# One routing group of eight units at the head of a fused attention and expert kernel

## The chip, the cores and the metric

The kernel runs on one core of a Trainium2 chip. The core has TensorE (PE, with its weight loads PEld), VectorE (DVE), ScalarE (ACT), GpSimd (POOL) and SyncE (SP); each takes its instructions in the order in which they are written, and waits for the others by semaphores. SP and POOL also issue DMAs. The metric is the device time of one execution, in microseconds (us).

## The reference

An attention with exponential gates over 4 x 8 sequences of 768 steps gives 3072 rows of 320; these go through a mixture of eight experts, two for each row.

```python
def _attn_ref(q, k, v, i_gate, f_gate, o_gate):
    ...
    for t in range(S):
        m_new = np.maximum(f_gate[:, :, t] + m, i_gate[:, :, t])
        f_stab = np.exp(f_gate[:, :, t] + m - m_new)
        i_stab = np.exp(i_gate[:, :, t] - m_new)
        ...
        y[:, :, t] = o * h_tilde / denom

def _moe_ref(x, w_gate, w_noise, noise, w1, w2):
    logits = x @ w_gate
    noise_scale = np.log1p(np.exp(x @ w_noise))
    noisy_logits = logits + noise_scale * noise
    top2 = np.argpartition(-noisy_logits, 2, axis=1)[:, :2]
    top2_l = np.take_along_axis(noisy_logits, top2, axis=1)
    top2_l = top2_l - top2_l.max(-1, keepdims=True)
    top2_w = np.exp(top2_l)
    top2_w /= top2_w.sum(-1, keepdims=True) + 1e-09
    ...
            h = np.maximum(x[mask] @ w1[e], 0.0)
            out[mask] += top2_w[mask, k, None] * (h @ w2[e])
```

## The kernel before

**Attention.** The steps are cut into chunks of 64 and the batch into two pairs, which makes 24 units of 128 rows. A loop with one iteration for each unit `i` (0 to 21; 22 and 23 are written out behind it) issues the work of several units at once: `k_part(i + 1)` (`kd`, L367), `c_part(i)` (the state, `st` L387, copied by L390), `o_part(i)` (L396), `e_part(i + 2)` (the gates' exponentials, `e` L336 and `w` L339), `f_part(i)` (`dn` L401 and L403, `tm` L407, then `xr` on GpSimd, L408), `p_part(i + 1)` (`p`, L373, or L377 where a sequence starts), `s_part(i + 2)` (L359), and for the unit before, the transposes L419, their copy L423 and the logits L439. `XR` rows are written to DRAM by `keep_rows`. In the same loop the first expert's weights come in: at the ends of iterations 11, 13, 17, 19, 20 and 21 ScalarE rounds a piece (`w1h`) and GpSimd subtracts it (`w1l`, L147).

**Routing.** `g_part(g)` is a generator that routes a group of units (four before). It starts when the group's last unit has its logits. Its steps: softplus of the noise (L542; three activations that `act` issues, L719; L551 to L561), noisy logits (L564), MAX8 for each unit (L569), the search of its indices for each unit (L572), one-hots (L579), counts (`m` L585, L588 or L590; `base` by a scan, L593), weights (L602, L604), and then, when TensorE has added the counts (`want`, `r_part`, L448 to L450), the rank of every row in its expert's list (L614, L630), split into a column `ai`, `ah` and a place `bi` (L634 to L642), and two tables of one-hot factors, `OA` (L649, L652) and `OB` (L655). A burst of eight matmuls (`b_part`, L459) multiplies these and adds them to the table `TBL` that says which rows an expert takes. `done` counts the units that are in it.

**What sets the order.** `fill` issues steps of the waiting generators, four times in an iteration: a little after `kd`, after each of the `dn` steps, and at the end up to a share of 1.6 for an iteration (a step counts as 0.19, MAX8 0.1, a search 0.15, the products 0.3, 0.3 and 0.6). `lag` says how many units later a burst or a count may be issued. When 12 units are in the table, `decode` (L473 to L490) makes row numbers of the first expert's first 384 places and `gather` (L803, GpSimd) fetches these rows in two iterations, two tiles and one. When 20 and 24 are in it, the same is done for the other places.

**Expert 0.** Behind the loop `mm1(0, 0, f)` runs for eight `f` (L1031), with routing in between by `advance`, and then three passes of 24 matmuls each into `sums` (L1154), eight for each of three tiles; `low_w2` (L1128) makes the low half of its second weights beside them. In the third pass the gathered tiles 3 and 4 are transposed (L833) for `mm1(0, 1, f)`. The other seven experts follow.

Of the kernel before, what the change touches and what calls it, by code (L numbers as in the profile page):

```python
# [10 lines left out]
HF = mybir.dt.float16  # L11
# [3 lines left out]
OP = mybir.AluOpType  # L15
# [3 lines left out]
NE, F, DM = 8, 1024, 320  # L19
# [8 lines left out]
TC = BLK // 128  # L28
# [5 lines left out]
FIT = 2048  # L34
FF = 1024
NM = 768
GROUPS = tuple((u, 4) for u in range(0, 24, 4))
GOF = {u: g for g, (u0, n) in enumerate(GROUPS) for u in range(u0, u0 + n)}
NB = 4

EF, LONG = 2, 3
NR = NE - EF
# [25 lines left out]
def build(ctx, tc, qk, vk, og, fi, noise, wgn, w1, w2, cst, ce, out):  # L68
    nc = tc.nc
    V, A, P, T, SP = nc.vector, nc.scalar, nc.gpsimd, nc.tensor, nc.sync  # L70
# [14 lines left out]
    spot = keep.tile([128, 128, 2], HF, name="spot")  # L85
    cols = keep.tile([128, NE * TC, 2], HF, name="cols")
    sgn = keep.tile([128, 2 * NU], HF, name="sgn")
# [422 lines left out]
    def lc_part(i, t, w):  # L510
        u = i - 2
        if 0 <= u < NU:
            g = GOF[u]
            c = u - GROUPS[g][0]
            if c == 0:
                LG[g] = rt.tile([128, NB, 16], F32, name="lg")
            A.activation(LG[g][:, c, :], t[:, LGC:LGC + 16], AF.Copy)
# [6 lines left out]
    anew = {}  # L524
    for nb in sorted({n for _, n in GROUPS}):
        anew[nb] = rt.tile([128, NE, nb + 1], BF, name=f"anew_{nb}", bufs=1)
        P.memset(anew[nb], 1.0)
        P.memset(anew[nb][:, :, 0], 0.0)
    bursts, done, acts, lag = [], [0], [], [1, 1]
    OBT = [rt.tile([128, 4, 128, 2], HF, name=f"ob{i}", bufs=1) for i in range(2)]  # L530
    OAT = [rt.tile([128, 4, NE * TC, 2], HF, name=f"oa{i}", bufs=1) for i in range(2)]

    def g_part(g):

        u0, nb = GROUPS[g]
        lg = LG[g][:, 0:nb]
        f = lambda a: a.rearrange("p u e -> p (u e)")
        fe = lambda a: a.rearrange("p e u -> p (e u)")
        sm = lambda name, shape, dt=F32: rt.tile(shape, dt, name=f"{name}_{nb}", bufs=1)
# [93 lines left out]
        ai = sm("ai", [128, 2 * nb], I32)  # L633
        V.tensor_scalar(ai, f(r), 7, None, op0=OP.arith_shift_right)  # L634
        yield
        n = 2 * nb
        assert n == 8
        bi = sm("bi", [128, n], HF)
        V.scalar_tensor_tensor(bi, ai, -128.0, f(r), op0=OP.mult, op1=OP.add)
        yield  # L640
        ah = sm("ah", [128, n], HF)
        V.tensor_copy(ah, ai)  # L642
        while done[0] < u0 - 4:
            yield "wait"
        OB, OA = OBT[g % 2], OAT[g % 2]
        C = NE * TC
        yield "long"
        two = lambda a, c: a.rearrange("p (a b) -> p a b", b=2)[:, :, None, :].to_broadcast([128, 4, c, 2])
        V.tensor_tensor(OA, cols[:, None].to_broadcast([128, 4, C, 2]), two(ah, C), op=OP.is_equal)  # L649
        yield 0.3  # L650
        yield "long"
        V.tensor_mul(OA, OA, two(sgn[:, 2 * u0:2 * u0 + n], C))  # L652
        yield 0.3
        yield "long"
        V.tensor_tensor(OB, spot[:, None].to_broadcast([128, 4, 128, 2]), two(bi, 128), op=OP.is_equal)  # L655
        yield 0.6
        bursts.append(([OB[:, j // 2, :, j % 2] for j in range(n)], [OA[:, j // 2, :, j % 2] for j in range(n)], unit[0] + lag[1]))
        if u0 + nb == NU:
            V.tensor_add(rk[:, 0:1], rk[:, 0:1], bump[0])
            yield  # L660
# [37 lines left out]
    spent, long = [0.0], set()  # L698
# [48 lines left out]
    def route(i):  # L747
        if 2 <= i <= NU + 1 and sum(GROUPS[GOF[i - 2]]) == i - 1:
            routing.append(g_part(GOF[i - 2]))
# [91 lines left out]
    unit = [0]  # L841
# [3 lines left out]
    while i < NU - LEAD:  # L845
# [33 lines left out]
        if i in (6, 7):  # L879
            n = slice(64 * (i - 6), 64 * (i - 6) + 64)  # L880
# [52 lines left out]
    u = NU - 2  # L933
# [19 lines left out]
    u = NU - 1  # L953
# [197 lines left out]
    for k, (l, r) in enumerate(((HH, W2H), (HLO, W2H), (HH, W2L))):  # L1151
        for n in range(24):
            t, j = divmod(n, 8)
# [261 lines left out]
```

## Time and profile before

| | |
|---|---|
| three executions | 512.7, 514.81, 516.75 us, median 514.81 |
| span of the profiled execution | 512.4 us (its own time outside the span is not recorded) |
| busy TensorE, VectorE, ScalarE, GpSimd | 97%, 65%, 48%, 45% of the span |
| granted TensorE clock | 0.986 |

The span runs from the first instruction to the last. Times in the rows are counted from its start. A busy share is an average over two stages: the attention loop takes the first 127 us, the experts the rest.

### The profile page before, as it was taken

How to read it: one execution, taken by the hardware profiler on the slowest of the kernel's cores; microseconds unless marked ns; L12 is line 12 of the kernel's file. 1: busy time of each engine (PE TensorE's matmuls, PEld its weight loads, DVE VectorE, ACT ScalarE, POOL GpSimd, SP SyncE). 2: the span in 40 equal slices, each digit the busy share in tenths (PEclk: the TensorE clock that was granted, in tenths of full speed). 3: DMA queues.
4: the chain of work that ended last, by engine and by line, in shares of the span. 5: the costliest groups of instructions: out<-in, count | busy, mean ns of one | idle time of the engine just before them, and what ended most of it. 6: DMA issues, size and time to landing. Idle time of an engine off the chain costs nothing.

```text
span 512.4 us, 13150 instructions
## 1 busy us (share of the span) xinstructions
PE 497.5 (97%) x5043; PEld 472.3 (92%) x5043; DVE 331.3 (65%) x935; ACT 245.7 (48%) x584; POOL 231.1 (45%) x303
## 2 busy tenths in 40 slices
PE   8899999998999999999999999999999999999995
PEld 4698888887999988999999999999999999999994
DVE  8868889889787586754853675375448347555410
ACT  7768888898623355423531543154235315514300
POOL 9736666265113876156135605531561354151033
PEclk9969999999999999999999999999999999999998
DMA  6888787877767465296159417723941682372033
GB/s 168 237 224 259 211 245 207 228 209 230 260 217 234 108 98 180 46 242 157 30 100 271 104 28 195 171 79 68 278 90 39 162 203 80 65 169 26 2 36 45
DMA packets 51493, 76.89 MB, mean 150 GB/s; under 512 B 10825, under 2 KB 41808, under 8 KB 51392
## 3 DMA queue, kind: packets, MB, share of 16 engines
q1 hardware_dynamic: 38576, 50.16, 33.7%
q0 software_dynamic: 12848, 25.82, 24.0%
q8 instruction: 42, 0.69, 0.6%
q14 instruction: 27, 0.22, 0.1%
HBM read 52.10 MB, written 17.32 MB: 135 GB/s over the span
## 4 chain that ended last, share of the span: by engine, by line
PE 83%; DVE 8%; DMA 4%; ACT 2%; issue 1%; POOL 1%; SPq 1%; POOLq 0%; DVEq 0%
PE s L1031 25%; PE e L1031 12%; PE o L1066 5%; PE o L1065 5%; PE o L1064 5%; PE st L1066 5%; PE st L1065 5%; PE st L1064 5%; PE o L396 3%; DVE p L373 2%; PE e L336 2%; PE s L359 1%; PE s L1154 1%; PE xt L439 1%; PE st L387 1%; DVE kd L367 1%
## 5 line engine op out<-in xcount | busy, mean ns | idle before, releaser
L1087 POOL DMA_INDIRECT y_out<-y,tok x53 | 87.2, 1646 | 178.6 <-DVE y L1077 177.5
L1044 ACT ACTIVATE hx<-s 128x384 fp32r<-128x384 f32 (+5 forms) x91 | 43.5, 478 | 72.7 <-PE s L1031 67.9
L1031 PE MATMUL s<-xh,w1h 128*128 128x384 f32 (+6 forms) x273 | 76.0, 336 | 0.0
L803 POOL DMA_INDIRECT xg<-rows,tok x53 | 56.3, 1062 | 35.7 <-issue 13.7
L1047 DVE SCALAR_TENSOR_TENSOR hx<-s,hx 128x384 fp32r<-128x384 f32 (+3 forms) x91 | 48.1, 528 | 34.2 <-ACT hx L1044 34.0
L1031 PE MATMUL s<-xh,w1l 128*128 128x384 f32 (+6 forms) x273 | 61.9, 334 | 0.0
L1066 PE MATMUL o<-w2h,hx 128*128 128x320 f32 x184 | 56.9, 309 | 0.0
L1064 PE MATMUL o<-w2h,hx 128*128 128x320 f32 x184 | 56.8, 309 | 0.0
L1065 PE MATMUL o<-w2l,hx 128*128 128x320 f32 x184 | 56.8, 309 | 0.0
L1066 PE MATMUL st<-w2h,hx 128*128 128x320 f32 x176 | 54.4, 309 | 0.0
L1064 PE MATMUL st<-w2h,hx 128*128 128x320 f32 x176 | 54.4, 309 | 0.0
L1065 PE MATMUL st<-w2l,hx 128*128 128x320 f32 x176 | 54.3, 309 | 0.0
L1031 PEld LDWEIGHTS s<-xh,w1h 128*128 128x128 f32 x273 | 48.8, 188 | 1.3 <-ACT xh L835 0.3
L1031 PEld LDWEIGHTS s<-xh,w1l 128*128 128x128 f32 x273 | 47.8, 188 | 1.1 <-DVE xh L837 0.2
L1031 PE MATMUL s<-xl,w1h 128*128 128x384 f32 (+6 forms) x182 | 46.0, 334 | 0.0
L1044 ACT ACTIVATE hx<-e 128x384 fp32r<-128x384 f32 (+5 forms) x45 | 21.7, 482 | 48.9 <-PE e L1031 36.2
L1077 DVE TENSOR_SCALAR y<-o,gw 128x320 f32<-128x320 f32 x23 | 12.7, 550 | 45.8 <-PE o L1066 45.8
L1077 DVE TENSOR_SCALAR y<-st,gw 128x320 f32<-128x320 f32 x22 | 12.1, 551 | 43.3 <-PE st L1066 43.3
L1031 PE MATMUL e<-xh,w1h 128*128 128x384 f32 (+6 forms) x135 | 38.4, 338 | 0.0
L408 POOL TENSOR_TENSOR xr<-tm,vk 128x320 f32<-128x320 f32 x24 | 20.9, 871 | 35.3 <-ACT w L339 10.4
L345 ACT ACTIVATE vk<-vk 128x320 f32<-128x320 f32 x72 | 33.8, 471 | 2.8 <-DMA vk<-og_in 1.9
L1064 PEld LDWEIGHTS o<-w2h,hx 128*128 128x128 f32 x184 | 34.5, 188 | 0.0
(247 smaller groups left out, 1242.1 us busy)
## 6 DMA issues: line engine op xcount, KB each, us to landing
raw<-w_in SPq DMA_DIRECT2D x6, 1280.0 KB, 6.9
qk<-qk_in SPq DMA_DIRECT2D x24, 256.0 KB, 3.9
raw<-w_in SPq DMA_DIRECT2D x6, 1024.0 KB
y_out<-zrow SPq DMA_DIRECT2D x15, 320.0 KB, 4.2
raw<-w_in SPq DMA_DIRECT2D x17, 256.0 KB, 7.7
vk<-vk_in POOLq DMA_DIRECT2D x24, 162.0 KB, 3.9
vk<-vk_in SPq DMA_DIRECT2D x24, 162.0 KB, 4.0
vk<-og_in SPq DMA_DIRECT2D x24, 160.0 KB, 3.6
```

The source lines that it names most:

```text
L345: A.activation(g, g, (AF.Exp, AF.Ln, AF.Exp)[p], bias=float(p == 1), scale=(-1.0, 1.0, -1.0)[p])
L396: T.matmul(OQ[u][half[p], h, :], PP[u][n, p, h, :], VK[u % 4][p][n, h * 41:h * 41 + 41], start=True, stop=True)
L408: P.tensor_mul(XR[u], tm.rearrange("p h d -> p (h d)"), SG[u % 4])
L803: P.indirect_dma_start(out=XG[0:rows_of(e, t), t], out_offset=None, in_=XD[0:n], in_offset=bass.IndirectOffsetOnAxis(ap=token(e, t), axis= ...
L1031: T.matmul(ps[:, 0:n], l, r, start=i == 0, stop=i == len(ops) - 1)
L1044: A.activation(hi, x, AF.Relu)
L1047: V.scalar_tensor_tensor(lo, top[0], 0.0, top[1].bitcast(F32), op0=OP.max, op1=OP.subtract)
L1064: T.matmul(ps, HH[:, j, c], W2H[:, j], start=j == 0, stop=False)
L1065: T.matmul(ps, HH[:, j, c], W2L[:, j], start=False, stop=False)
L1066: T.matmul(ps, HLO[:, j, c], W2H[:, j], start=False, stop=j == 7)
L1077: V.tensor_scalar(y[0:n], ps[0:n], GW[e][0:n, t:t + 1], None, op0=OP.mult)
L1087: st = P.indirect_dma_start(out=out, out_offset=bass.IndirectOffsetOnAxis(ap=token(e, t), axis=0), in_=y[0:n], in_offset=None, compute_op= ...
```

## The change

The first eight units become one group. Its steps are issued once, on tiles twice as wide; MAX8 and the search stay one for each unit. The tables `OA` and `OB` are still made for four units at a time, so the group makes two pairs and two bursts, and the second half waits until its buffer is free. Groups after the first are as before. The tile of logits (`lg`) is eight units wide for all groups.

```diff
-GROUPS = tuple((u, 4) for u in range(0, 24, 4))
+GROUPS = ((0, 8), (8, 4), (12, 4), (16, 4), (20, 4))
 GOF = {u: g for g, (u0, n) in enumerate(GROUPS) for u in range(u0, u0 + n)}
-NB = 4
+NB = 8
...
-        while done[0] < u0 - 4:
-            yield "wait"
-        OB, OA = OBT[g % 2], OAT[g % 2]
...
+        C, n = NE * TC, 8
         two = lambda a, c: a.rearrange("p (a b) -> p a b", b=2)[:, :, None, :].to_broadcast([128, 4, c, 2])
...
+        for uh in range(u0, u0 + nb, 4):
+            while done[0] < uh - 4:
+                yield "wait"
+            OB, OA = OBT[uh // 4 % 2], OAT[uh // 4 % 2]
+            own_ = slice(2 * (uh - u0), 2 * (uh - u0) + n)
+            yield "long"
+            V.tensor_tensor(OA, cols[:, None].to_broadcast([128, 4, C, 2]), two(ah[:, own_], C), op=OP.is_equal)
+            yield 0.3
+            yield "long"
+            V.tensor_mul(OA, OA, two(sgn[:, 2 * uh:2 * uh + n], C))
+            yield 0.3
+            yield "long"
+            V.tensor_tensor(OB, spot[:, None].to_broadcast([128, 4, 128, 2]), two(bi[:, own_], 128), op=OP.is_equal)
+            yield 0.6
+            bursts.append(([OB[:, j // 2, :, j % 2] for j in range(n)], [OA[:, j // 2, :, j % 2] for j in range(n)], unit[0] + lag[1]))
```

VectorE, iteration 13, from `tm` of unit 13 on; before:

```order
L407 SCALAR_TENSOR_TENSOR tm<-dn,o 128x320
L373 TENSOR_TENSOR p<-s,w 128x1024
L655 TENSOR_TENSOR ob_217<-spot,bi_1641 128x1024
L542 SCALAR_TENSOR_TENSOR na_1741<-lg 128x32
L367 TENSOR_TENSOR kd<-vk_114,w 128x640
L401 RECIPROCAL dn<-o 128x8
L551 SCALAR_TENSOR_TENSOR co_1806<-t_4_1744,ue_1743 128x32
L403 SCALAR_TENSOR_TENSOR dn<-dn 128x8
```

and in the changed kernel:

```order
L407 SCALAR_TENSOR_TENSOR tm<-dn,o 128x320
L373 TENSOR_TENSOR p<-s,w 128x1024
L614 TENSOR_TENSOR oh_1479<-oh_1479,rk_1531 128x128
L630 TENSOR_REDUCE rank<-oh_1479 128x16
L634 TENSOR_SCALAR ai_1674<-rank 128x16
L637 SCALAR_TENSOR_TENSOR bi_1676<-ai_1674,rank 128x16
L640 CAST ah_1678<-ai_1674 128x16
L649 TENSOR_TENSOR oa_221<-cols,ah_1678 128x448
L652 TENSOR_TENSOR oa_221<-oa_221,sgn 128x448
L655 TENSOR_TENSOR ob_219<-spot,bi_1676 128x1024
L367 TENSOR_TENSOR kd<-vk_114,w 128x640
L542 SCALAR_TENSOR_TENSOR na_1696<-lg 128x32
```

The rank and the first half of the tables of the wide group stand there now, and the next group's first step stands behind `kd`.

TensorE, the passes into `sums` behind the attention; `ob` are the burst's factors of units 16 to 19. Before:

```order
L1154 MATMUL s_3008<-w2h,hx 128x320 x8
L1154 MATMUL s_3009<-w2h,hx 128x320 x8
L1154 MATMUL e<-w2h,hx 128x320 x8
L1154 MATMUL s_3008<-w2h,hx 128x320 x4
L459 LDWEIGHTS ob_216
L459 MATMUL o<-oa_218,ob_216 128x56
```

and in the changed kernel:

```order
L1154 MATMUL s_2962<-w2h,hx 128x320 x8
L1154 MATMUL s_2963<-w2h,hx 128x320 x8
L1154 MATMUL e<-w2h,hx 128x320 x8
L1154 MATMUL s_2962<-w2h,hx 128x320 x8
L1154 MATMUL s_2963<-w2h,hx 128x320 x8
L1154 MATMUL e<-w2h,hx 128x320 x2
L459 LDWEIGHTS ob_219
L459 MATMUL o<-oa_221,ob_219 128x56
```

The burst stood behind 4 matmuls of the second pass; now it stands behind 18.

VectorE at the same place, from that burst's `ob` to the decode. Before:

```order
L655 TENSOR_TENSOR ob_216<-spot,bi_3000 128x1024
L561 TENSOR_TENSOR ln_2934<-ln_2934,nzt 128x32
L564 TENSOR_TENSOR nl_3033<-ln_2934,lg 128x32
L569 MAX mx_3035<-nl_3033 128x8 x4
L466 TENSOR_TENSOR tbl<-tbl,o 128x56
```

and in the changed kernel:

```order
L655 TENSOR_TENSOR ob_219<-spot,bi_2956 128x1024
L561 TENSOR_TENSOR ln_2904<-ln_2904,nzt 128x32
L564 TENSOR_TENSOR nl_2991<-ln_2904,lg 128x32
L1128 TENSOR_TENSOR w2l<-raw_122,w2h 128x320 x3
L569 MAX mx_3012<-nl_2991 128x8 x3
L1128 TENSOR_TENSOR w2l<-raw_122,w2h 128x320
L466 TENSOR_TENSOR tbl<-tbl,o 128x56
```

Four subtractions for `w2l` stand ahead of the addition to the table now.

## Rows read from the trace of the kernel before

**Rows 1.** The page, the chain of work that ended last, by engine.

```profile
PE 83%; DVE 8%; DMA 4%; ACT 2%; issue 1%; POOL 1%; SPq 1%; POOLq 0%; DVEq 0%
```

**Rows 2.** Stretches: start:end, length, busy time of each engine (instructions), clock, DMA.

```profile
43.74:49.74 6.00, 5.93 (x126) 5.06 (x124) 4.27 (x12) 5.42 (x18) 3.83 (x7) 1.00 0.86 237
49.74:72.84 23.10, 22.23 (x531) 20.07 (x530) 19.55 (x74) 18.90 (x52) 16.03 (x32) 1.00 0.84 231
72.84:83.24 10.40, 9.73 (x233) 8.52 (x235) 9.88 (x31) 8.35 (x22) 6.86 (x12) 1.00 0.78 217
83.24:88.00 4.76, 4.53 (x119) 4.20 (x119) 4.53 (x9) 4.44 (x13) 2.71 (x3) 1.00 0.71 219
88.00:111.54 23.54, 23.14 (x573) 20.73 (x575) 20.48 (x81) 20.14 (x55) 9.91 (x15) 1.00 0.79 207
111.54:117.47 5.93, 5.09 (x122) 4.43 (x126) 5.83 (x18) 4.54 (x12) 5.30 (x6) 1.00 0.94 292
117.47:126.87 9.40, 8.31 (x217) 7.37 (x210) 8.99 (x20) 8.83 (x22) 5.38 (x6) 1.00 0.68 196
126.87:155.87 29.00, 29.00 (x234) 27.77 (x232) 22.18 (x106) 14.53 (x43) 6.49 (x10) 1.00 0.69 224
```

**Rows 3.** Chain of waits: start, time on the chain, what; two neighbouring `o` bursts.

```profile
38.09 0.93 PE o L396 x32
...
42.49 0.93 PE o L396 x32
```

**Rows 4.** VectorE's groups, 39.34 to 126.87: busy us, mean ns, idle before.

```profile
L373 DVE TENSOR_TENSOR p<-s,w 128x1024 f32<-128x1024 f32 x18 | 21.9, 1216 | 0.0
L367 DVE TENSOR_TENSOR kd<-vk,w 128x640 f32<-128x640 f32 x16 | 12.9, 809 | 0.0
L407 DVE SCALAR_TENSOR_TENSOR tm<-dn,o 128x320 f32<-128x320 f32 x18 | 8.5, 473 | 1.0
...
L655 DVE TENSOR_TENSOR ob<-spot,bi 128x1024 f16<-128x1024 f16 x4 | 2.7, 682 | 0.0
...
L649 DVE TENSOR_TENSOR oa<-cols,ah 128x448 f16<-128x448 f16 x4 | 1.6, 392 | 0.1
...
L553 DVE RECIPROCAL na<-t 128x32 f32<-128x32 f32 x4 | 1.4, 345 | 0.0
...
L579 DVE TENSOR_TENSOR oh<-cs,mi 128x64 f32<-128x64 f32 x4 | 0.9, 221 | 0.0
...
L551 DVE SCALAR_TENSOR_TENSOR co<-t,ue 128x32 f32<-128x32 f32 x4 | 0.8, 192 | 4.2 <-ACT t L719 4.1
L557 DVE TENSOR_TENSOR ln<-ln,co 128x32 f32<-128x32 f32 x4 | 0.8, 192 | 0.4
```

**Rows 5.** VectorE's timeline: start, duration, instruction; two of the four long ones.

```profile
75.52 1.28 DVE L585 TENSOR_TENSOR m<-oh 128x32 bf16<-128x32 f32 x1
...
113.44 2.25 DVE L575 TENSOR_TENSOR d<-mx 128x4 f32<-128x4 f32 x1
```

**Rows 6.** GpSimd's timeline, three of the six subtractions; idle before in brackets.

```profile
75.41 1.28 POOL L147 TENSOR_TENSOR w1l<-raw,w1h 128x512 fp32r<-128x512 f32 x1 [0.81 <-ACT w1h L144]
...
85.50 1.36 POOL L147 TENSOR_TENSOR w1l<-raw,w1h 128x512 fp32r<-128x512 f32 x1 [0.49 <-ACT w1h L144]
...
104.51 1.56 POOL L147 TENSOR_TENSOR w1l<-raw,w1h 128x512 fp32r<-128x512 f32 x1 [1.14 <-ACT w1h L144]
```

**Rows 7.** TensorE's timeline in the passes into `sums`.

```profile
148.12 0.39 PE L459 MATMUL o<-oa,ob 128*128 128x56 f16 x8
148.34 2.01 PE L1154 MATMUL s<-w2h,hx 128*128 128x320 f32 x12
...
153.56 0.49 PE L833 MATMUL s<-cs,xg 128*128 128x128 f32 x3
```

**Rows 8.** GpSimd's timeline: the first gather for tiles 3 and 4.

```profile
150.00 1.03 POOL L803 DMA_INDIRECT xg<-rows,tok  x1 [10.12 <-DVE km L490]
```

**Rows 9.** DMA issues, 149.5 to 153: kind, count, median us from issue to landing.

```profile
xg<-rows,tok POOLq DMA_INDIRECT x2, 3.0
```

More of the change, by code (lines that the diff above doesn't have):

```diff
@@ L635, in g_part @@
         yield
-        n = 2 * nb
-        assert n == 8
-        bi = sm("bi", [128, n], HF)
+        bi = sm("bi", [128, 2 * nb], HF)
         V.scalar_tensor_tensor(bi, ai, -128.0, f(r), op0=OP.mult, op1=OP.add)
         yield
-        ah = sm("ah", [128, n], HF)
+        ah = sm("ah", [128, 2 * nb], HF)
         V.tensor_copy(ah, ai)
-        while done[0] < u0 - 4:
-            yield "wait"
-        OB, OA = OBT[g % 2], OAT[g % 2]
-        C = NE * TC
-        yield "long"
-        two = lambda a, c: a.rearrange("p (a b) -> p a b", b=2)[:, :, None, :].to_broadcast([128, 4, c, 2])
[L649 to L657, printed above, removed]
+        C, n = NE * TC, 8
+        two = lambda a, c: a.rearrange("p (a b) -> p a b", b=2)[:, :, None, :].to_broadcast([128, 4, c, 2])
+        for uh in range(u0, u0 + nb, 4):
[13 more added lines that the diff above has]
+            bursts.append(([OB[:, j // 2, :, j % 2] for j in range(n)], [OA[:, j // 2, :, j % 2] for j in range(n)], unit[0] + lag[1]))
         if u0 + nb == NU:
```

## Prediction

> **What bounds the kernel now.** I read the chain of waits first, by engine: 83% of the span is TensorE and 8% VectorE [rows 1]. Nearly all of the TensorE part lies in the expert stage; the VectorE part lies in the attention loop, and there alone the change moves work. So next I cut the loop into its iterations, each from the step `dn` of one unit to that of the next, and read length and busy time by engine [rows 2]. Iterations 5 to 21 take 83.13 us, 4.89 each, and VectorE is busy for 73.5 of these, TensorE for 79.0, ScalarE for 70.6. What an iteration costs when nothing but TensorE sets it is seen ahead of the first group: from one `o` burst to the next in the chain, 38.09 to 42.49, 4.40 us [rows 3]. So at most 83.1 - 17 x 4.40 = 8.3 us, 1.6% of the span, can be had in the loop. The groups of instructions then tell what fills VectorE: `kd` 0.81, `p` 1.22, `tm` 0.47 and two small ones (some 0.35) belong to each unit, about 2.85; the rest is routing, dozens of instructions of some 0.2 us that hardly grow with their width [rows 4]. Behind the loop TensorE is busy for all of 29.00 us [rows 2], and routing shows only where it waits for gathered rows.
>
> **What goes away.** Two groups of four become one of eight. The eight MAX8, the eight index searches and the six table products stay; some twenty small instructions go once. By their rows they go from about 0.15 to 0.345 (the reciprocal), 0.2 on average [rows 4]: 4.0 us. Those that stay get wider. 128x32 takes 0.192 and 128x64 takes 0.221, so a doubled width costs 0.03 to 0.07, and the reciprocal, which is long for its width, about 0.2: together 0.7. Durations overlap at their ends by some 6% (they add to more than their stretch), so VectorE has about 3.1 us less to do. Where it is the engine that ends last, that is gain; where TensorE's 4.40 ends last, it is not.
>
> The Trainium skill (Perfetto Trace Analysis, section Optimizing Scalar/DVE Operations) says just this: a fixed cost per instruction is saved by larger operations if the engine is saturated. By it the whole 3.1 us would come off. The trace agrees on the cost; whether the engine is saturated is what the next part takes iteration by iteration.
>
> **What moves.** The first group can start only when eight units have logits: at the end of iteration 9, not 5. Iterations 6 to 8 then hold no routing, and VectorE idles in them; 9 to 21 hold it all. I put down for each iteration the larger of 4.45 (the floor with a little slip) and the work that the new order gives it, without the collisions of the next part:
> - Iteration 5: 6.00 today. VectorE waits in it for the group's first activations, part of the 4.1 us that the first step after them waits in all [rows 4], and ScalarE is busy 5.42 [rows 2]. The two activations that it waits for go (some 0.45), the one-time copies stay: 5.55.
> - Iterations 6 to 10: 23.10 today. Three at the floor, 13.35. Then 9 with the start of the group and its wait for ScalarE, as today's 9: 4.75. And 10, with the 128x64 forms: 4.6. Sum 22.7.
> - Iterations 11 and 12: 10.40. All eight index searches but none of the rank stand in 11: 5.0; 12 has little: 4.45. Sum 9.45.
> - Iteration 13: 4.76 today, with one table product and the next group's first step. It now gets the rank, both small casts, both products of one half and the long one: 2.85 of its own, 0.3 and 0.3 for the 128-wide product and its reduction (a 64-wide one is 0.22), 0.5 for three small ones, 0.39, 0.39, 0.68 [rows 4], 0.2 for the next group. 5.6, less the 6%: 5.3.
> - Iterations 14 to 18: 23.54. The second half's table in 14 makes it 4.75, then 4.45 and 4.65. In 17 and 18 the first step after the activations stands behind `p` now and no longer waits for them: 4.65 and 4.75. Sum 23.25.
> - Iteration 19: 5.93, nearly all of it one collision. Without: 4.9, with the decode of the first 12 units, that comes here from 18.
> - Iterations 20 and 21: 9.40. Now 9.0, since the last six steps for units 12 to 15 fall out of the loop, some 1.9 us.
>
> Sum 80.15 for 83.13: **3.0 us less**, a third of which is the idle stretch being short and most of the rest the wait in 17 and the missing collisions.
>
> **Collisions.** Four times in the loop a tiny VectorE instruction takes one to two us: `m` 1.28 at 75.52 where a wider product takes 0.22, `d` 2.25 at 113.44 [rows 4, 5]. Each lies under a subtraction on GpSimd, the low half of the early weights, 75.41 to 76.69 for the first [rows 6]. Each reads two tiles or one tile twice, none from PSUM; the forms that read one tile or PSUM are never long.
>
> The Trainium skill (SBUF — State Buffer, section Who interferes with whom) has the rule: a VectorE instruction with two SBUF inputs and a GpSimd one that reads SBUF share a read port, and whichever comes second waits until the first is done. The four stalls agree. By it the loop's time would hang on which instructions stand beside the six subtractions.
>
> So I go through the new order for what stands beside them, by the rows' own pattern. The subtractions stay at the ends of the same iterations (11, 13, 17, 19, 20, 21). In 11 the index searches, with one tensor input, will stand there, and `kd` behind them, which may have to wait 0.5. In 13 it comes at 85.50 [rows 6], 2.26 after the iteration's start, and `tm` and `p` are over by 1.9; there `bi` will wait, 0.7. In 17 it starts while `kd` runs [rows 6], and behind `kd` the next group's first step now stands in place of a reciprocal out of PSUM: 1.1. In 19 the searches come first, then the one-hot and the decode: 0 to 1.2. In 20 the step is `dn` as before: 0.3 on the path. Bounds: nothing, and 3.8 for all. Since neither end has a row for the new order I take the middle, 1.9: the loop comes to 82.05, **1.1 less**.
>
> **Behind the loop.** The group of units 12 to 15 is half an iteration later, and by their due units the bursts of matmuls that add to the table move. The one that completes 20 units stood after 4 matmuls of the second pass of `sums`, at 148.12; now it stands after 18. Twelve of them take 2.01 less the pipelined end, 0.147 each [rows 7]: 14 x 0.147 = 2.06 us later. Behind it hang the addition to the table, the decode, the gathers on GpSimd (first issued 150.00 [rows 8], landing 3.0 after [rows 9], so 153.0) and the transposition that TensorE reads at 153.56 [rows 7]. Slack 0.56; so TensorE stands 2.06 - 0.56 = **1.5 us**, where today it has no gap. VectorE now also issues four subtractions for `w2l` ahead of that addition; I get them done by the time the burst lands, and if they aren't, it is up to 1.4 more. Least: a landing 0.6 faster, 0.9. The last burst keeps its place. The gather of the third tile comes one iteration later as well, and lands about a us before its transposition, no cost. The write of the weights for eight units is one DMA for two, beside the loads on SP's queue: the same bytes.
>
> **Sum.** -1.1 in the loop, +1.5 behind it: +0.4 on a span of 512.4. The median of the three runs is 514.81, 2.4 above that span; I carry the difference over: **515.2 us**.
>
> **Rivals.**
> - *All of the saving arrives*: the collisions fall on searches and reciprocals, 3.0 in the loop, 0.9 behind it: -2.1, 512.7. It is what the Trainium skill's grouping rule (Perfetto Trace Analysis, above) would have. For it: VectorE is over 95% busy in 13 and 19. Against: the light iterations sit at TensorE's floor. Chance 0.24. Only if the heavy ones also came near 4.40 would it be over 1%, below 509.7: 0.06 of it.
> - *Slower by the late gather*: one mechanism, the table of 20 units. All collisions stay (3.8 - 3.0 = +0.8 in the loop), the four subtractions hold the addition back, 1.5 + 1.4 behind: +3.7, 518.5. It decides once the gather's slack of 0.56 is used up, and the order of instructions uses it up. Chance 0.26, 0.08 of it over 1%, if the third tile's gather is late too.
> - *The loop isn't VectorE's at all*: ScalarE is busy nearly as long as VectorE [rows 2]; then only the wait in iteration 5 goes and the result is 514.81 - 0.5 + 1.5 = 515.8, not to be told from my forecast; it is in its 0.50.
>
> That the merged steps are not made is excluded by the order of instructions.
>
> **How the numbers follow.** Forecast 0.50, gain 0.24, loss 0.26. 1% is 5 us, about what a measurement of this kernel can tell from no change. Faster by over that 0.06, slower 0.08, within 0.86. The range leaves out a tenth on each side: from 510.7, the full saving less half the spread of the three runs (2.0), to 518.6, the loss.
>
> **What would show it.** In the profile after: no routing on VectorE in iterations 6 to 8, and these at 4.4 to 4.5; iterations 13, 17 and 19 above 5; twenty small VectorE instructions fewer; stalls of over 1 us under the GpSimd subtractions, and which; ahead of the first transposition in the third pass a gap on TensorE of 1 to 2 us. I am wrong if that gap isn't there (then by 1.5 to the fast side), or if iterations 6 to 8 stay at 4.6 because of another engine.

## The result and the profile after

| | before | changed |
|---|---|---|
| median of 19 executions each | 513.98 us | 518.59 us |
| ratio to before | | 1.0076, 95% interval 1.0057 to 1.0095 |
| span of the profiled execution | 512.4 us | 516.3 us |
| granted TensorE clock | 0.986 | 0.993 |
| VectorE instructions | 935 | 915 |

The change costs 3.9 us by the ratio, and 3.9 by the two spans. The ratio leaves out four slow executions of the changed kernel (522.3 to 603.2 us), so it lies below the quotient of the two medians. The range, 510.7 to 518.6, held the median by 0.01 us, which is luck; the likeliest value, 515.2, lies 3.4 below it. The twenty instructions are gone, and nothing came of it.

The chain of the changed kernel, by engine, answers to [rows 1]: VectorE's share falls from 8% to 4%, but TensorE's rises.

```profile
PE 85%; DVE 4%; ACT 3%; POOL 3%; issue 2%; DMA 2%; SPq 1%; POOLq 0%; DVEq 0%; ACTq 0%
```

The stretches of [rows 2], cut again from `dn` to `dn`, each 0.24 us ahead of the unit's second `dn` step (iterations 5; 6 to 8; 9; 10; 11 and 12; 13; 14 to 18; 19; 20 and 21; then the stage behind the loop, to the transposition in the third pass):

```profile
42.02:46.42 4.40, 4.40 (x112) 4.00 (x113) 3.97 (x10) 3.89 (x12) 2.22 (x4) 1.00 0.99 275
46.42:59.96 13.54, 13.48 (x334) 12.03 (x335) 9.60 (x15) 12.06 (x32) 11.23 (x22) 1.00 0.90 245
59.96:67.12 7.16, 6.06 (x122) 5.37 (x122) 2.34 (x6) 4.91 (x13) 3.78 (x7) 1.00 0.97 264
67.12:71.81 4.69, 3.51 (x75) 3.20 (x74) 4.35 (x16) 3.05 (x9) 2.26 (x4) 1.00 0.47 105
71.81:80.60 8.79, 8.13 (x216) 7.21 (x215) 8.62 (x39) 7.40 (x19) 6.40 (x10) 1.00 0.74 220
80.60:87.29 6.69, 6.69 (x141) 5.78 (x145) 6.33 (x15) 5.64 (x15) 3.61 (x6) 1.00 0.86 225
87.29:111.57 24.28, 22.46 (x564) 20.19 (x555) 21.80 (x72) 19.57 (x54) 8.86 (x14) 1.00 0.76 209
111.57:117.93 6.36, 4.14 (x116) 3.64 (x115) 5.41 (x29) 4.04 (x11) 3.71 (x5) 1.00 0.89 261
117.93:127.84 9.91, 9.19 (x226) 8.15 (x227) 6.95 (x17) 8.95 (x22) 5.58 (x7) 1.00 0.57 160
127.84:156.40 28.56, 27.43 (x220) 26.26 (x219) 23.96 (x110) 13.69 (x41) 5.68 (x8) 1.00 0.68 223
```

Iterations 5 to 21 take 85.80 us (127.82 - 42.02) where before they took 83.13. Iterations 5 to 8 are 1.9 faster; 9, 13 and 19 are far above. In 9 and 19 no engine is busy throughout: VectorE has 2.34 of 7.16 us, TensorE 4.14 of 6.36. So it isn't work that makes them long. From one profile to the other the whole 3.87 us is: prologue to iteration 5 -1.48 (the granted clock was lower there in the profile of before), loop +2.67, from its end to the passes into `sums` +0.58, the first two passes with the gap +1.31, the third pass +0.19, the seven experts +0.60.

**TensorE stops inside a burst.** TensorE's timeline around both long iterations; in brackets, the idle time before a row and what ended it:

```profile
63.19 0.28 PE L396 MATMUL o<-vk,p 104*64 104x41 f32 x2
64.57 1.13 PE L396 MATMUL o<-vk,p 128*64 128x41 f32 x30 [1.10 <-issue]
...
114.27 1.13 PE L396 MATMUL o<-vk,p 128*64 128x41 f32 x30
117.62 0.26 PE L396 MATMUL o<-vk,p 128*64 128x41 f32 x2 [2.22 <-issue]
```

It stands after 2 of 32 matmuls of one burst and after 30 of another: all 32 read the same tiles and write the same one, as the first two already did, and "issue" says that no semaphore ended the wait. So it is not a wait for data. Counting TensorE's own instructions (matmuls and weight loads) from the program's start gives the clue:

```
stop before instruction   remainder by 256   16,384-byte packet began, landed   TensorE went on
2498 (1.10 us)            194                 61.98   63.22                      64.57
4801 (2.22 us)            193                115.18  116.16                     117.62
```

The two are 9 x 256 apart, less one missing record. The DMA records hold a packet of 16,384 bytes on TensorE's instruction queue every 256 instructions (64 bytes each). Mostly it has landed when some 100 instructions are left; here one at most was, and TensorE went on 1.35 and 1.46 us behind the landing. The engine had run out of program. The same shows at all 29 stops of this kind in the loops of this case, in 11 kernels: TensorE went on 1.2 to 1.6 us after a packet had landed. The Trainium skill (Runtime: NRT & Kernel Launch, section Instruction fetch mechanics) states these blocks of 16 KiB or 256 instructions, and that their cost is mostly hidden; the trace agrees on the size, and here 3.3 us were not hidden.

**One wait now counts for more.** VectorE, iteration 9:

```profile
65.73 0.21 DVE L401 RECIPROCAL dn<-o 128x8 f32<-128x8 f32 x1 [3.50 <-PE o L396]
67.22 0.23 DVE L551 SCALAR_TENSOR_TENSOR co<-t,ue 128x64 f32<-128x64 f32 x1 [1.28 <-ACT t L719]
67.37 0.16 DVE L403 SCALAR_TENSOR_TENSOR dn<-dn 128x8 f32<-128x8 f32 x1
```

The group's first step after its activations stands between the halves of `dn` and waits 1.28 us for ScalarE; `tm`, `p` and the next burst of `o` stand behind it (TensorE idles 1.18 there). It stood and waited so before, but TensorE lost only 0.69 (VectorE, then TensorE, before):

```profile
68.25 0.19 DVE L551 SCALAR_TENSOR_TENSOR co<-t,ue 128x32 f32<-128x32 f32 x1 [1.22 <-ACT t L719]
...
70.35 1.13 PE L396 MATMUL o<-vk,p 104*64 104x41 f32 x32 [0.69 <-issue]
```

**Collisions.** VectorE's rows beside four subtractions, and two of these, answering to [rows 5, 6]:

```profile
75.31 1.27 DVE L367 TENSOR_TENSOR kd<-vk,w 128x640 f32<-128x640 f32 x1
...
84.78 1.77 DVE L655 TENSOR_TENSOR ob<-spot,bi 128x1024 f16<-128x1024 f16 x1
...
104.44 1.35 DVE L649 TENSOR_TENSOR oa<-cols,ah 128x448 f16<-128x448 f16 x1
...
115.36 1.63 DVE L367 TENSOR_TENSOR kd<-vk,w 128x640 f32<-128x640 f32 x1 [0.22 <-issue]
```

```profile
74.62 1.27 POOL L147 TENSOR_TENSOR w1l<-raw,w1h 128x512 fp32r<-128x512 f32 x1 [0.81 <-DMA vk<-vk_in]
84.70 1.30 POOL L147 TENSOR_TENSOR w1l<-raw,w1h 128x512 fp32r<-128x512 f32 x1 [2.08 <-ACT w1h L144]
```

Against their own shortest (0.79 for `kd`, 0.68, 0.38) they lose 0.48 + 1.09 + 0.97 + 0.84 = 3.4 us. These are other instructions than before: the stalls moved with the order. They cost VectorE less than before, where four instructions (1.28, 1.26, 2.25 and 1.07 us) lost 5.1 against the shortest of their like.

**Behind the loop**, answering to [rows 7 to 9] (TensorE; GpSimd; the gathers' landing):

```profile
151.85 0.39 PE L459 MATMUL o<-oa,ob 128*128 128x56 f16 x8
...
156.64 0.55 PE L833 MATMUL s<-cs,xg 128*128 128x128 f32 x3 [1.23 <-DMA xg<-rows,tok]
```

```profile
153.63 1.03 POOL L803 DMA_INDIRECT xg<-rows,tok  x1 [10.05 <-DVE mx L569]
```

```profile
xg<-rows,tok POOLq DMA_INDIRECT x1, 3.0
```

The burst, the gather and the gap stand where they were forecast: 153.63 + 3.0 lands at 156.63, and TensorE has waited 1.23 us for it.

### The profile page after: what moved, and what is told of

Same layout as the page of the kernel before. It is cut to its first block, busy times and chain, and to the rows that moved or that the text cites. A ratio compares the mean times of both kernels' runs of the same rounds, so it can differ in the third digit from the quotient of the medians.

```text
span 516.3 us, 13112 instructions
## 1 busy us (share of the span) xinstructions
PE 493.7 (96%) x5040; PEld 469.7 (91%) x5040; DVE 329.5 (64%) x915; ACT 245.0 (47%) x579; POOL 229.7 (44%) x304
## 4 chain that ended last, share of the span: by engine, by line
PE 85%; DVE 4%; ACT 3%; POOL 3%; issue 2%; DMA 2%; SPq 1%; POOLq 0%; DVEq 0%; ACTq 0%
PE s L1031 24%; PE e L1031 12%; PE o L1066 5%; PE o L1065 5%; PE o L1064 5%; PE st L1066 5%; PE st L1065 5%; PE st L1064 5%; PE o L396 3%; PE s L359 2%; PE e L336 2%; PE st L387 2%; PE xt L439 2%; PE xt L419 1%; PE s L1154 1%
## 5 line engine op out<-in xcount | busy, mean ns | idle before, releaser
L803 POOL DMA_INDIRECT xg<-rows,tok x53 | 55.1, 1041 | 35.2 <-issue 14.0
L396 PE MATMUL o<-vk,p 128*64 128x41 f32 (+2 forms) x768 | 29.7, 233 | 7.2 <-issue 4.9
```

The lines of the kernel that those rows point to most:

```text
L396: T.matmul(OQ[u][half[p], h, :], PP[u][n, p, h, :], VK[u % 4][p][n, h * 41:h * 41 + 41], start=True, stop=True)
L803: P.indirect_dma_start(out=XG[0:rows_of(e, t), t], out_offset=None, in_=XD[0:n], in_offset=bass.IndirectOffsetOnAxis(ap=token(e, t), axis= ...
```

## Experiments

Below, "loop" is iterations 5 to 21, and "stops" are TensorE's idle times of over 0.2 us in it in front of an instruction whose number leaves 192 to 194 by 256, with no semaphore. TensorE's clock is granted at one of two levels, 2.4 and 1.2 GHz; a granted clock of 0.50 is the lower one. The first four were timed on a chip where before took 526.04 us (517.46 to 532.28). In all four traces there the first rows of the experts come 7 to 11 us later behind the passes into `sums`, and the granted clock is 0.50 in a part of that time; of these runs the traces tell more than the times.

**The burst of 20 units due earlier** (changed kernel):

```diff
-    lag[:] = 10, 9
+    lag[:] = 10, 3
```

> The changed kernel with the bursts asked in the passes into sums due after 3 steps, not 9, so that the one that completes 20 units stands behind 6 matmuls of the second pass (4 before the change, 18 in it). If the late table is what TensorE waits for ahead of the transposition (gap 1.23 us in the changed kernel), that gap goes and the time falls by 1.2 to 2 us against the changed kernel, so to about 1.004 of the kernel before. Rival, that the wait comes from late steps of the group of units 12 to 15 on VectorE: the burst then waits for its own factors, the gap only moves ahead of the burst, and nothing is gained.

Ratio 1.0034 (0.9971 to 1.0097). The first two passes with what follows, to the transposition, take 9.69 us (11.04 in the changed kernel, 9.73 before): the gap is gone, and the burst's late place was its cause. The loop was 88.74 here, although its program is that of the changed kernel. It has stops of 0.40, 1.65 and 0.69, the last two at the changed kernel's places (2497 and 4800 here), and behind the longest the clock fell to 0.50:

```profile
67.97:81.62 13.65, 13.65 (x186) 12.43 (x184) 9.06 (x43) 7.72 (x20) 5.54 (x9) 0.50 0.51 148
```

The third tile's transposition, at 133.42, waited 1.09 for its gather.

**No GpSimd subtractions**, in both kernels; `w1l` is cleared in their place, so the low half of expert 0's first weights is left out:

```diff
-                P.tensor_sub(W1L[n, k, s], RAW1[n, k, s], W1H[n, k, s].bitcast(F32))
+                P.memset(W1L[n, k, s].bitcast(F32), 0.0)
```

> The changed kernel with each of the six early subtractions on GpSimd put in by a memset of the same tile (the low half of the first expert's early weights is zero then, for its time only). If VectorE's long instructions are collisions of two engines that both read SBUF, none of over 0.5 us beyond its like is left at these places (a memset reads nothing), iterations 11, 13, 17 and 19 fall from 5.1, 6.7, 5.6 and 6.4 by some 0.4, 1.1, 1.3 and 0.9, and the time falls by up to 3.5 us against the changed kernel. Rival, TensorE out of instructions because the DMA engines are full: the loop still stops inside two bursts of matmuls, 1 to 2 us each, and the time falls by less than 2 us.

> The kernel before with the same memsets in place of the six subtractions. Collisions: its four long instructions (1.28, 1.26, 2.25, 1.07 us) go, some 3 us of the loop with them, ratio about 0.994. If the collisions cost the kernel before as much as the changed one, they explain nothing of the difference between the two; if the changed one gains 1 us or more beyond this, they are a part of it.

Ratios 0.9996 (0.9920 to 1.0072) and 1.0074 (1.0012 to 1.0135). GpSimd's rows are now

```profile
82.56 0.52 POOL L147 MEMSET w1l<- 128x512 f32 x1
```

and no VectorE instruction beside them is long. In the changed kernel iteration 11 falls from 5.12 to 4.80, 13 from 6.69 to 5.58, 17 from 5.58 to 4.74; so the collisions are real. But the loop stays at 85.92: the stops grow to 3.90 (six of them), and 6.8 us of it run at 0.50 of the clock. Before's loop falls from 83.13 to 81.10, without a stop. So the collisions cost before 1.7 to 2.0 us (its one stop is 0.31), and iterations 11, 13 and 17 of the changed kernel 2.3; what holds the loop up without them is the stops and the lower clock. The time doesn't show it: before's ratio was expected at 0.994, and nothing here says why it is 1.0074.

**TensorE's program shifted by half a block** (changed kernel; 128 TensorE instructions ahead of everything):

```diff
     wp = psum.tile([128, 512], F32, name="o")
+    for _ in range(64):
+        T.matmul(wp[:, 0:2], wz[:, 0:128], wz[:, 0:2], start=True, stop=True)
```

> The changed kernel with 64 matmuls of two columns ahead of the first warm ones, in time in which TensorE waits for its first data: 128 more instructions, so that the blocks of 256 in which TensorE's instructions are fetched begin elsewhere in the program. If the two stops inside bursts of o (1.1 us at 63.5, 2.2 us at 115.4, 2304 instructions apart) are late fetches, they move by about half a unit or go, and the time differs from the changed kernel's by 1 to 3.5 us, more likely downward. Rival, a wait for data at these places: they stay where they are in the program, and the time stays within 0.5 us.

TensorE's timeline (lines are 3 higher behind the edit):

```profile
41.43 0.47 PE L387 MATMUL st<-vk,kd 128*40 128x41 f32 x9 [2.33 <-issue]
...
100.47 0.27 PE L359 MATMUL s<-qk 64*64 64x64 f32 x2 [0.55 <-issue]
```

These are instructions 1472 and 4032, both of remainder 192, inside a burst of `st` and one of `s`. At the work where the changed kernel stopped there is no stop. Where TensorE stops hangs on its instruction count, not on the work there. Ratio 1.0199 (1.0073 to 1.0326), where a fall had been held more likely. The loop is 85.55 although its stops add up to 0.55 only: behind the stop of 2.33, which lies ahead of iteration 5, the granted clock is 0.50 from 41.6 to 48.4, and iteration 5 takes 6.65. There is also a wait of 2.57 in expert 0.

**More DMA in the kernel before**, to bring the stop about there:

```diff
+        if i == 9:
+            SP.dma_start(XG[:, 4:7, 0:DM], w2[0, 0:384].rearrange("(j p) c -> p j c", p=128))
```

> The kernel before, with one load of 491 KB more at the head of iteration 9 (rows of the second weights, to a tile that is cleared afterwards; nothing else changes, and no engine waits for it but the clearing on GpSimd). The theory that TensorE's stops inside a burst of `o` are late packets of its own program, held up by full DMA engines: the packet that is due at instruction 2497 of TensorE, in iteration 9 or 10, comes late in this kernel as it did in the changed one: a stop of 0.5 to 2 us at an instruction number whose remainder by 256 is 192 or 193, with no semaphore behind it, in a kernel that has none there. The rival, that such stops come from the new order of the instructions: no stop of over 0.3 us at 2497; only waits for the late units (on `st` or `o` by semaphore) by some 1 us.

Missed: no stop at 2497. The load did not fill the engines when that packet was due (share 0.76 in 56 to 60 us; the packet began at 59.3 and landed with some 150 instructions left). But late in the loop they were full, and there this kernel of the old order has a stop too, before instruction 5058 (remainder 194): first the stretch, in which a part is at the lower clock, then TensorE's row:

```profile
112.00:120.00 8.00, 6.40 (x130) 5.73 (x126) 7.31 (x20) 5.57 (x15) 4.45 (x6) 0.79 1.04 271
```

```profile
122.19 0.64 PE L419 MATMUL xt<-cs,xr 128*128 128x128 f32 x2 [1.06 <-issue]
```

The kernel before has a share of 0.95 in the same stretch and no stop there. 515.27 us in one execution, before 514.57.

**Loads of the early weights moved** (changed kernel):

```diff
-W1LD, W1AT, W2AT = (6, 9, 12, 15, 18), (11, 13, 17, 19, 20, 21), 21
+W1LD, W1AT, W2AT = (6, 10, 12, 14, 16), (11, 13, 17, 19, 20, 21), 21
```

> The changed kernel, with three of the five loads of the first weights at other iterations: the second at 10 in place of 9, the fourth at 14 in place of 15, the fifth at 16 in place of 18; the bytes are the same. Late packets behind full DMA engines: the stop at instruction 2497 (1.10 in the changed kernel) falls below 0.5, iteration 9 (7.16) comes below 5.5, and the one at 4801 (2.22) falls below 1; stops may show at other instructions with remainder 192 or 193 where the loads now are. The rival, that the stops hang on the regrouped order: both stay, 1.0 and 2.0 within 0.5, at the same instructions.

In 56 to 60, 60 to 64 and 112 to 116 us the DMA share is 0.85, 0.77 and 0.65 (changed kernel 1.03, 0.98 and 0.94). The stop at 2498 shrinks from 1.10 to 0.28, that at 4801 is gone; iteration 9 is still 6.34, where less than 5.5 was expected; that is the wait for ScalarE. The loop is 82.53. But the time is 517.43 us, hardly less (one execution), for TensorE now waits at the third gathered tile:

```profile
128.14 0.52 PE L833 MATMUL st<-cs,xg 128*128 128x128 f32 x3 [1.84 <-DMA xg<-rows,tok]
```

**The subtractions in quarters** (changed kernel):

```diff
-                P.tensor_sub(W1L[n, k, s], RAW1[n, k, s], W1H[n, k, s].bitcast(F32))
+                for c in range(f, f + 512, 128):
+                    q = slice(c, c + 128)
+                    P.tensor_sub(W1L[n, k, q], RAW1[n, k, q], W1H[n, k, q].bitcast(F32))
```

> The changed kernel, with each of the six subtractions for `w1l` on GpSimd written as four of 128 columns. The theory that VectorE's long instructions wait for the one GpSimd instruction that runs: no VectorE instruction waits longer than one quarter, some 0.4 us, so `kd`, `oa` and `ob` beside the subtractions stay below 1.2 where they took 1.27, 1.35, 1.63 and 1.77; iterations 11, 13 and 17 lose 0.3 to 1 each, the loop 2 to 3 us as long as TensorE's own stops don't grow; ratio to before 1.000 to 1.005. The rival, that the two only share bandwidth: the sum of the delays stays, about 3.4 us, and with it the loop.

Ratio 1.0135 (1.0081 to 1.0189), far above what was expected. VectorE beside the quarters of iteration 13 (lines are 2 higher), then GpSimd:

```profile
86.47 0.95 DVE L657 TENSOR_TENSOR ob<-spot,bi 128x1024 f16<-128x1024 f16 x1
87.34 1.07 DVE L369 TENSOR_TENSOR kd<-vk,w 128x640 f32<-128x640 f32 x1
88.33 0.44 DVE L544 SCALAR_TENSOR_TENSOR na<-lg 128x32 f32<-128x32 f32 x1
```

```profile
86.39 2.75 POOL L149 TENSOR_TENSOR w1l<-raw,w1h 128x128 fp32r<-128x128 f32 x4 [1.79 <-ACT w1h L144]
```

No delay is over 0.4, as expected, but more instructions are delayed, these three by 0.27, 0.27 and 0.26: iteration 13 is 6.39 against 6.69, and 11 and 17 lose 0.06 and 0.15. Over the loop the delays add up to 2.7 against 3.4, so the rival was nearly right about the sum: small turns saved little. The loop is 84.92 with 2.75 of stops; the third tile waits 1.92.

**Quarters, loads and burst together** (changed kernel; the three edits above).

> The changed kernel with the subtractions in quarters, the loads at 6, 10, 12, 14 and 16, and the burst that completes 20 units due 6 matmuls into the second pass (lag 3 in place of 9). If what the change loses is made of the collisions (about 2 to 3 us), TensorE's late program packets (3 us) and the gap before the transposition (1.3 us), it is ahead of before by 2 to 4 us: ratio 0.992 to 0.998, the loop below 82 us, no gap before the third pass. If late packets only come elsewhere, the loop stays at 83 to 85 and the ratio at 1.000 to 1.004.

Ratio 1.0089 (1.0053 to 1.0125); a gain was expected. There are no stops, the loop is 81.05, as expected, and the gap ahead of the third pass is gone (9.66). All of it is lost between. TensorE, then the stretches behind the loop:

```profile
126.83 0.52 PE L835 MATMUL st<-cs,xg 128*128 128x128 f32 x3 [2.78 <-DMA xg<-rows,tok]
```

```profile
123.29:126.83 3.54, 0.76 (x7) 0.55 (x7) 2.30 (x7) 1.89 (x5) 1.42 (x2) 1.00 0.63 157
126.83:130.45 3.62, 3.62 (x45) 3.21 (x45) 0.72 (x3) 2.28 (x6) 2.56 (x5) 0.65 0.52 175
130.45:136.00 5.55, 5.55 (x26) 5.55 (x27) 3.19 (x11) 1.67 (x6) 0.86 (x1) 0.61 0.54 185
```

The third tile's gather is waited for 2.78 us, and after that the granted clock is 0.65 and 0.61, so in part at the lower of its two levels, 1.2 GHz: 9.17 us for work of 3.62 x 0.65 + 5.55 x 0.61 = 5.7 at full clock, 3.4 more if all of it went with the clock (an estimate). From the loop's end to the passes into `sums` it is 23.22; less both, 17.0, before's 16.95.

**The third gather with the first two** (changed kernel with the moved loads and the earlier burst):

```diff
-            gather(0, 0, tiles(0, 0)[late:late + 2])
-            late += 2
+            gather(0, 0, tiles(0, 0)[late:late + 3])
+            late += 3
```

> The changed kernel with the loads of the first weights at iterations 6, 10, 12, 14 and 16, the burst that completes 20 units due 6 matmuls into the second pass, and the third tile's gather issued with the first two (one iteration earlier). The theory that the third tile's gather is late as soon as the loop runs without TensorE's stops (waits of 1.84, 1.92 and 2.78 in the kernels with other loads or quarters, none in the changed kernel, whose loop ends later): no wait ahead of the transposition of the third tile, loop 82 to 83.5, from its end to the passes into `sums` 16.5 to 17.5, the third pass without a gap; ratio 0.996 to 1.002. The rival, that the transposition waits for something else (the DMA engines' traffic there): a wait of over 1 us stays in front of the transpositions and the ratio is at 1.004 or above.

Ratio 1.0052 (1.0011 to 1.0093). GpSimd's last of three gathers, and TensorE at the third tile:

```profile
117.63 1.66 POOL L803 DMA_INDIRECT xg<-rows,tok  x1 [0.30 <-issue]
```

```profile
126.23 0.55 PE L833 MATMUL st<-cs,xg 128*128 128x128 f32 x3 [0.46 <-ACT vk L390]
```

No wait for a gather is left, and none ahead of the third pass (9.66): the theory of the late gather holds. But the loop is 84.83, with stops of 2.52 although its loads lie as in the kernel without any, and with 3.4 us at 0.50 of the clock behind the last of them; that expectation failed, and the ratio with it.

**That kernel, with the group's step two places later**:

```diff
         while acts:
             yield "wait"
+        if u0 == 0:
+            yield "wait"
+            yield "wait"
         co = sm("co", [128, nb, NE])
```

> As the kernel with the three gathers together, and the first group's first step after its activations two places later, behind `p` of unit 10 and not between the two halves of `dn`. The theory that this step's wait for ScalarE (1.28 in the changed kernel) stands on the path there: iterations 9 and 10 together lose about 1.2 (some 9.3 to 9.8 in place of 10.5 to 11), the gap of 1.18 ahead of the next burst of `o` goes, loop 81 to 82.3; with the other three repairs ratio 0.993 to 0.999, the fastest of all. The rival, that the wait is covered by TensorE's own work: 9 and 10 stay at 10.5 and the ratio is that of the kernel with the three gathers.

VectorE in iteration 9:

```profile
65.03 0.21 DVE L401 RECIPROCAL dn<-o 128x8 f32<-128x8 f32 x1 [2.40 <-PE o L396]
65.27 0.17 DVE L403 SCALAR_TENSOR_TENSOR dn<-dn 128x8 f32<-128x8 f32 x1
```

Nothing stands between the halves of `dn`, TensorE's gap of 1.18 is gone, and iterations 9 and 10 take 9.87 (10.44 with quarters, loads and burst, also without a stop): the wait was on the path, but worth some 0.6 rather than the 1.2 expected. Ratio 1.0021 (0.9990 to 1.0052): not ahead of before. A stop of 1.22 came back at instruction 4546, and the clock fell with it; the loop is 84.72.

```profile
108.65:115.47 6.82, 6.27 (x73) 5.53 (x75) 5.20 (x28) 3.11 (x8) 1.16 (x2) 0.50 0.61 185
```

**That edit alone** (changed kernel):

> The changed kernel with one edit: the first group's first step after its activations stands two places later, behind `p` of unit 10. The theory that its wait of 1.28 for ScalarE is on the path: the stop of TensorE of 1.18 ahead of the burst of `o` in iteration 10 goes, iterations 9 and 10 together come to 10.6 or less (11.85 in the changed kernel), the loop to 84.0 to 84.8; the gap in the third pass stays at 1.2; ratio 1.003 to 1.007. The rival, that the wait only fills what TensorE's stop leaves open: 9 and 10 stay above 11.4.

Iterations 9 and 10 come to 10.42, the loop to 83.43, both as expected or better; the stops fell to 1.38. But TensorE waits 1.1 for the third tile's gather in the loop's wake and 1.2 in the third pass, and the ratio, 1.0124 (1.0064 to 1.0184), is no better than the changed kernel's and misses the 1.003 to 1.007.

**Loads and step in the kernel before** (the step for the group of units 4 to 7, which starts in iteration 9 there).

> The kernel before with two of the same repairs: the loads at 6, 10, 12, 14 and 16, and the step after the activations two places later for the group that starts in iteration 9 (units 4 to 7). It tells what these edits are worth without the regrouping. If the kernel before already hides late program packets and that wait: loop 82.5 to 83.3, ratio 0.998 to 1.002. If the repairs help any order of the work: loop below 82, ratio 0.994 to 0.998, and the regrouping has no part in what the kernel with all repairs gains.

511.55 us beside 512.94, ratio 0.9971 (0.9940 to 1.0001); loop 81.06, no stop, full clock. The repairs shorten the old order's loop by 2.1 us, at least as much as the new one's; the gain in time is not clear of noise. In the same comparison the regrouped kernel with all of them took 515.01.

## Why the prediction was right, and where it was wrong

The time stayed within 1%, as held likeliest, but it is up by 3.9 where 0.4 was forecast, and the mechanism that the text held likeliest for a loss (the late gather for 20 units) is only a third of the loss.

- *What goes away, what moves.* Right. Twenty instructions fewer; no routing in 6 to 8 (fifteen VectorE instructions, five each), and these at 4.73, 4.40 and 4.41. Iteration 5 came out at the floor, 4.40, not 5.55: without the group's activations, its one-time copies cost nothing. VectorE's busy time in the loop fell from 73.5 to 69.4 us. The shorter collisions make 1.8 of that, so about 2.4 went with the instructions, where 3.1 was forecast. The overlap of durations was taken as 6%; in the trace of before it is 13% (89.2 us of durations in 77.4 busy, 39.34 to 126.87).
- *Collisions.* The mechanism and the form of its victims held, and the term, 1.9 from 0 to 3.8, was under-sized: the delays add up to 3.4, and 2.3 came back in iterations 11, 13 and 17 when the subtractions went. In 13 `ob` was hit for 1.09, not `bi` for 0.7. One reading was too simple: the instruction of 2.25 us at 113.44 [rows 5] began 0.95 ahead of its subtraction (114.39), beside GpSimd's product for `xr` (113.57 to 114.44), which reads two tiles as well.
- *The loop, -1.1.* **This is the step that failed.** It measured +2.67. Loop less stops is, in the changed kernel and its variants:

```
                                 loop    stops   difference   at half clock
changed kernel                   85.80   3.52    82.28         0
loads moved                      82.53   0.28    82.25         0
quarters                         84.92   2.75    82.17         0
quarters, loads, burst           81.05   0.00    81.05         0
loads, burst, three gathers      84.83   2.52    82.31         3.4
step alone                       83.43   1.38    82.05         3.4
without subtractions             85.92   3.90    82.02         6.8
loads, burst, gathers, step      84.72   1.22    83.50         6.8
program shifted                  85.55   0.55    85.00         4.5
burst earlier                    88.74   2.74    86.00        13.7
before                           83.13   0.31    82.82         0
before, without subtractions     81.10   0.00    81.10         0
before, loads and step           81.06   0.00    81.06         0
before, more DMA                 86.00   1.34    84.66         6.8
```

  (us; the last column is the part of the loop at a granted clock of 0.50.) The forecast for the loop was 82.05. The changed kernel, at full clock throughout, comes within 0.3 us of it if a stop costs its whole length, and so do two of its three variants at full clock: the miss is TensorE's late program, of which the text had no word.

  The rows far above have a part at the lower clock, and what that costs can be read off twice. Iterations 9 to 12 take 24.88 us with the burst earlier and 20.65 in the changed kernel, whose program is the same there: 3.7 beyond the longer stop. Iterations 18 to 21 take 22.27 with all repairs and 18.57 with the loads moved: 2.5 beyond the stop. Less these, the two loops are at 82.3 and 81.0. So a stop can cost more than its length. Ahead of every such part TensorE had stood for 0.8 to 2.3 us, but the changed kernel's stop of 2.22 was followed by none; which stops the lower clock follows is not shown.

  The parts of the sum are less good than the sum, too: 9 with 10 was costed at 9.35 and is 10.75 without the stop, since the wait for ScalarE, taken "as today", is on the path once VectorE no longer comes late to it (moving it gave back 0.6 to 0.9); iteration 5's 1.15 and 11 with 12 (8.79, where 9.45 stood without collisions) paid for that.
- *Behind the loop, +1.5.* Right: 1.23 of gap, and 1.31 by the length of the passes. It goes with the burst's place, as four kernels show. The four subtractions ahead of the addition didn't hold it back: from the burst's start to the gather 1.78 us pass (153.63 - 151.85), before 1.88. What was not in the sum is 0.58 from the loop's end to the passes, 0.19 behind the gap, 0.60 in the seven experts, and the 1.48 that the prologue was shorter.
- *Third tile's gather, no cost.* Right in this run, and by luck: it was issued at 124.66 and landed 3.8 later, 0.3 ahead of its transposition at 128.72. In the four kernels with a shorter loop that kept this gather's place (loads moved, quarters, both with the burst, the step alone), TensorE waited 1.1 to 2.8 for it, which is why taking the stops away alone gained almost nothing. A long loop is no safeguard, though: with the burst earlier (88.74) and the program shifted (85.55) it waited 1.09 and 1.38.
- *The grouping rule as a rival.* It does not hold here: VectorE was not the engine to end last in the light iterations (busy 9.60 of 13.54 us in 6 to 8), as the text argued.

What stays open: why the regrouped order meets more stops (0 to 3.9 us a run) than the old one (0 to 1.3). Each kernel has one profiled execution; the changed kernel and the one with the burst earlier have the same program in the loop, and the two largest stops stand at the same places in both, but with 1.10 and 2.22 us in one and 1.65 and 0.69 in the other. In the changed kernel the DMA engines were full when the two packets were due, and where their share fell, the stops went. But the same loads gave 0 and 2.5 us in two kernels, forcing a stop in the old order failed at its place, and a stop of 0.48 came in a stretch with a DMA share of 0.44 (104.60 to 108.07, three gathers together). That TensorE ran out of program is shown by the count, the shift and the packets; what holds a packet up is not.

## What to carry to other kernels

Time freed on an engine is worth only what the next chain leaves: here each repair handed its gain to another late thing (program packets, then a gather, then the clock behind that gather's gap or behind a stop). Before moving work in a tight loop, list the slack of each DMA that the end of the loop waits for, and cost the case in which the loop gets faster, not only slower. When a bottleneck engine stands inside a burst of like instructions without a semaphore, count its instructions: a remainder that repeats says that the program itself came late.

## What the runs showed of the hardware

- TensorE's instructions came in packets of 256, and its stops at a packet's edge were 0.2 to 2.3 us long, going on 1.2 to 1.6 us behind the landing of a packet at all 29 in the loops. The profile's name for them is "issue".
- Splitting each GpSimd subtraction of 1.3 us into four took what VectorE lost to them in the loop from 3.4 to 2.7 us only, while a GpSimd clear of the same tile, 0.52 us, delayed nothing.
- One gap of 2.78 us on TensorE was followed by 9.2 us at a mean granted clock of 0.63, which cost more than the gap. A stop of 1.65 us was followed by 13.7 us at 0.50, which cost 3.7; one of 2.22 us was followed by none.
